# A planned attention and gated-FFN kernel: one constant per rule of the order replaced by tables indexed by score visit

## The chip, the cores and the metric

The kernel runs on one core of a Trainium2 chip. The metric is the time of one execution in device microseconds (us). Shorter is better. The kernel before has a median of 1091.6 us over three runs (1091.21 to 1092.62).

## The reference

One transformer block on 2048 tokens with 1024 features, all in bf16: multi-query attention (32 query heads of 32 features that share one key and one value head), then a feed-forward network (FFN) with a sigmoid gate.

```python
xn = layernorm(x)
q = (xn @ wq).reshape(B, S, 32, 32).transpose(0, 2, 1, 3)   # 32 heads of 32
k, v = xn @ wk, xn @ wv                                      # one head of 32
p = softmax(einsum("bhqd,bkd->bhqk", q, k) * 32 ** -0.5)
h = x + einsum("bhqk,bkd->bhqd", p, v).transpose(0, 2, 1, 3).reshape(B, S, 1024) @ wo
hn = layernorm(h)
out = h + (sigmoid(hn @ w_gate) * (hn @ w_up)) @ w_down      # 1024 -> 3584 -> 1024
```

## The kernel before, in words

**Tiles.** Tokens are cut into 16 tiles of 128 rows. Attention handles a token tile in two halves of 16 heads each, called `hf` in the code, so there are 32 halves. For each half the 2048 keys are cut into 16 key tiles `kt`. One pair (half, key tile) is a *score visit*; there are 512 of them (`NV`), counted by `v`.

**One visit** (`emit_S`). TensorE runs four matmuls of 32x128 by 32x512, each on its own quarter of the rows of the array. They put the scores of 16 heads into a pair of pairs of PSUM banks of the tile `S_ps`. ScalarE then runs two exponentials of 128x1024 from `S_ps` into a buffer `Pr` (L707). `S_ps` holds three such half-visits, so the scores of visit v cannot start before an exponential of the visit before has ended: the third matmul of a visit waits for the first exponential of the visit before, the first one for the second exponential of the visit before that. So TensorE can run ahead of ScalarE by one visit and no more.

**What follows a visit.** VectorE adds the exponentials of a half up in `acc` (L680). TensorE multiplies the exponentials with the values in two *P V bursts* per half of eight key tiles each (`mk_PV`), four matmuls at a time on the four quarters of the columns. At the end of a half it forms the sums of the exponentials in one burst of 32 short matmuls (`mk_SUM`), again on quarters of the columns. The sums are inverted, written to DRAM and read back spread out (`r_scratch`, `rb`), multiplied in (`OT`), and after two halves the token tile goes through the output projection `OP`, the second layernorm, a DMA transpose into `hnT`, the gate and up matmuls `GU` (14 groups of 8 matmuls, weights streamed from DRAM in slabs), a tanh on ScalarE per gate group (L989; the sigmoid is written with tanh), and the down projection `D` (56 matmuls, weights resident). All these use the whole array. At the start there are also the transposes `xT`, the key and value projection `KV`, and the query projection `Q0`, `Q1`, `Q`.

**Modes of the array.** The planner calls the scores "row" mode, P V and sums "col" mode, and everything else "dense" mode. A *switch* is a change of mode between two neighbouring matmuls.

**What sets the order.** No engine chooses anything at run time. Before the program is written, a planner in the file (class `Plan` and the loop at the end of the kernel) simulates all engines with a cost for each instruction (`t_act`, `t_dve`, `SWITCH`, DMA rates) and writes a fixed list of instructions for every engine, with semaphore waits between them. At each step of simulated time the loop decides what TensorE does next:

1. If the next visit can start (`s_known`) and ScalarE has less than `run` = 700 ns of work queued, the visit is issued. This interrupts whatever group of matmuls is under way.
2. Right after a col matmul, if the next visit can start within `swait` = 400 ns, TensorE is left idle until then.
3. A long dense group (`LONG`) may be put aside for a P V, SUM, OP or hT group, if at least `rmin` = 900 ns of it are left or another condition holds. P V and SUM may begin only in row mode, that is right after a visit, or where buffers are short (`in_row`, with `pv_few` = 4 and `sum_few` = 0).
4. Otherwise the next matmul of the current group is issued, or a new group is taken from the queues in a fixed order of classes (`PRIOS[qf]`, or `PRIO_D` when a down projection is due).

`early` = 240 ns in `s_known` says how far ahead of the end of an exponential the visit may be issued. The lists of VectorE, GpSimd and of the DMA queue on SyncE come out of the same simulation, so a different decision on TensorE moves the instructions of all engines.

Of the kernel before, what the change touches and what calls it, by code (L numbers as in the profile page):

```python
# [15 lines left out]
SEM = 75.0  # L16


TUNE = dict(early=240, look=500, ln_v=1, warm=70, late=300, ws0=1, ws1=1, parts0=3, parts1=4, lord=2, h_ord=2,
            ho=3, ho2=0, pvl1=0, pvl2=0, col_ok=0, pace0=310, swait=400, parts=2, raw=1, rl=0, nd=2, pc=16,  # L20
            rate=315, pace=265, xd=4, qf=1, dall=1, wo_late=1, nkn=3, few=0, rmin=900, hmin=1, h0=100, h1=250,
            hf=1.35, run=700, sum_few=0, pv_few=4, d_off=0, d_a=-1, d_b=1, eb=450, eq=1500)


class Op:
# [131 lines left out]


def t_act(n):
    return dict(occ=n / 1.2 + 58.0, lat=n / 1.2 + 186.0 + SEM)  # L160


def t_dve(n, rate=0.96, fix=158.0):
# [3 lines left out]
SWITCH = 108.0  # L167


def bass_sequential_preLN__grouped_kv_mqa__glu_gated_glu__prompt_kernel(  # L170
# [12 lines left out]
    Bsz, S, D = A_x.shape  # L183
# [3 lines left out]
    NT = S // P  # L187
# [14 lines left out]
    with ExitStack() as es:  # L202
# [66 lines left out]
        pl = Plan()  # L269
# [169 lines left out]
        queues = collections.defaultdict(collections.deque)  # L439
        PRIO_D = ["xT", "KV", "Q0", "PV", "SUM", "OP", "hT", "D", "GU", "Q1", "Q"]  # L440
        head = [["xT", "KV", "Q0"], ["KV", "Q0", "xT"], ["Q0", "KV", "xT"], ["KV", "xT", "Q0"]][TUNE["h_ord"]] + ["PV", "SUM", "OP", "hT"]
        PRIOS = [head + ["GU", "D", "Q1", "Q"], head + ["Q1", "Q", "GU", "D"], head + ["Q1", "GU", "Q", "D"]]

        def mm(o, l, r, start, stop, **kw):
            return lambda: PE.matmul(o, lhsT=l, rhs=r, start=start, stop=stop, **kw)  # L445

        def pe_op(fn, n, mode, deps, last_of_round=True):
            if mode != pl.pe_mode:
                pl.free["pe"] += SWITCH
                pl.pe_mode = mode  # L450
            if mode == "dense":
                occ = max(25.0, n / 2.4 + 2.4)
            else:
                occ = max(25.0, n / 2.4 + 2.4) - 10.5 if last_of_round else 3.5
            return pl.op("pe", fn, deps, occ=occ, lat=max(25.0, n / 2.4 + 2.0) + 170.0 + SEM)
# [49 lines left out]
        k_ev, v_ev = {}, {}  # L505
# [118 lines left out]
        NV = len(visits)  # L624
# [31 lines left out]
        def s_known(v, t):  # L656

            sd = s_ready(v)
            return sd is not None and known(sd, t) and (v < 1 or known([exps[2 * v - 2]], t + TUNE["early"]))

        late_adds = collections.defaultdict(list)
        RAW = tuple(range(TUNE["raw"])) + ((NH - 1,) if TUNE["rl"] else ())
# [60 lines left out]
        PARTS = [(), (), (0, 8, 16), (0, 5, 10, 16), (0, 6, 11, 16), (0, 4, 8, 12, 16), (0, 7, 16), (0, 6, 16), (0, 4, 10, 16), (0, 4, 8, 16)]  # L723

        def parts_of(hf):
            return PARTS[TUNE["parts" if hf > 1 else "parts0" if hf == 0 else "parts1"]]

        rb_ld = {}
        rs_ev = {}
# [2 lines left out]
        oun_ev = {}  # L732

        def in_row(few):
            return v_done[0] >= NV or pl.pe_mode == "row" or len(free_slots) <= few or TUNE["col_ok"] and pl.pe_mode == "col"

        def mk_SUM(hf):
            a = acc[:, hf % 2, :]

            def atoms(b):  # L740
                return [(mm(F_ps[DH * j:DH * (j + 1), b, 0:64], sel[:, bb, :], a[:, j * 512 + bb * 64:j * 512 + (bb + 1) * 64],
                            bb == 0, bb == 7, tile_position=(0, DH * j)), 64, "col" if j == 3 else "col-", [])
                        for bb in range(8) for j in range(4)]

            def after(b, last):
                sum_last[hf] = last
                flush_adds(hf + 2)
                rc = pl.op("dve", lambda: DVE.reciprocal(r_sb[:, :], F_ps[:, b, 0:64]),
                           [last, rd_ld.get(hf - 1)], prio=0, occ=480, lat=560 + SEM)
                rd_ld[hf] = dma(lambda: SP.dma_start(r_dram, r_sb[0:P:4, :]), "rd", 8192, [rc] + (rb_ld[hf - 1] if hf - 1 not in RAW else []), prio=0)  # L750
                rb_ld[hf] = [dma(lambda j=j: SP.dma_start(
                    rb[DH * j:DH * (j + 1), :], bass.AP(r_dram.tensor, r_dram.offset + 512 * j, [[0, DH], [1, 512]])),
                    "rb", 65536, [rd_ld[hf], ot_ev.get(hf - 1), ot_ev.get(0)], prio=0) for j in range(4)]
                finish(hf)
                return [rc]
            return Group("SUM", atoms, lambda: [add_op.get((hf, NT - 1)), c_sel], after, lambda: in_row(TUNE["sum_few"]))

        def finish(hf):

# [13 lines left out]
        def mk_PV(hf, part, sums=False):  # L773
# [36 lines left out]
                        finish(hf)  # L810
                return [oun_ev[(hf, part)]]

            lag = TUNE["pvl2"] if final else TUNE["pvl1"]

            def first():
                return [exp_of[(hf, kt, i)] for kt in kts[:len(kts) - lag] for i in range(2)] + [c_one if sums else v_ev.get(kt) for kt in kts]

            def gate():
                if part == 0 and hf >= 2 and not (hf - 2 in ot_ev and known([ot_ev[hf - 2]], pl.free["pe"])):
                    return False  # L820
                if sums and part == 0 and hf >= 2 and hf - 1 not in ot_ev:
# [25 lines left out]
        v_done = [0]  # L847
# [239 lines left out]
        def all_done(v):  # L1087

            v_done[0] = v
            if v == NV:  # L1090
                all_S[0] = True
                pl.t_last = pl.free["pe"]
                load_next([(s.rearrange("p (d f) -> p d f", d=4), rel) for s, rel in free_slots])

        def known(deps, t):
            return all(d is not None and d.end is not None and d.end <= t for d in deps)

        while True:
            t = pl.free["pe"]
# [203 lines left out]
```

## Time and profile before

| what | value |
|---|---|
| median of three runs | 1091.6 us |
| the profiled execution, span from first to last instruction | 1092.9 us, 1.3 us above the median |
| TensorE matmul busy | 1060.6 us, 97% |
| TensorE weight loads busy | 439.3 us, 40% |
| ScalarE busy | 1000.7 us, 92% |
| VectorE busy | 848.9 us, 78% |
| DMA queue busy share | 74.1% of 16 engines, 233.70 MB |
| first exponential starts, last one ends | 14.17 us, 1009.88 us |

No time of the profiled execution other than its span is given, so the span stands for it. The run has three stages. Up to about 140 us the projections run beside the first 64 visits. From about 200 us to the last exponential the trace repeats itself every 62.1 us, which is one token tile: 32 visits, one pass of the FFN, one output projection. After the last exponential comes a tail of 83.0 us without scores, with the rest of the FFN of two tiles and all of it for the last.

In the profile, PE is TensorE, PEld its weight loads, ACT ScalarE, DVE VectorE, POOL GpSimd, SP SyncE. A line such as `646.07 2.12 PE L445 MATMUL F_ps<-ring,hnT ... x9` of the timeline reads: from 646.07 us, 2.12 us long, nine matmuls with their source and target. The recorded length of one 512-column matmul (379 to 385 ns) includes the way through the array; the next one starts 216 ns after it, so costs are read from start to start.

### The profile page before, as it was taken

To read this page: it belongs to the slowest core of one execution; us is meant where nothing else is said; L and a number is where in the kernel's file an instruction comes from. 1 tells how busy PE (TensorE), PEld (TensorE's weight loads), DVE (VectorE), ACT (ScalarE), POOL (GpSimd) and SP (SyncE) were. 2 spreads that over 40 slices of the span, in tenths; PEclk is the share of its full clock that TensorE was granted. 3 is DMA by queue.
4 is the path that set the end of the run, shared out by engine and by line. 5 is a ranking of instruction groups with operands and counts; after the bars stand their busy time and mean duration, and the time that the engine had idled before them with its cause. 6 is when DMAs were issued, how large, how long until landed. Compare 5 with 4: busy or idle time off the path is not lost.

```text
span 1092.9 us, 23470 instructions
## 1 busy us (share of the span) xinstructions
PE 1060.6 (97%) x9314; PEld 439.3 (40%) x9454; DVE 848.9 (78%) x1054; ACT 1000.7 (92%) x1152; POOL 39.5 (4%) x61
## 2 busy tenths in 40 slices
PE   8999999999999999999999999999999999999998
PEld 6533465333333333333333333333333333333485
DVE  8989988787887878787887878787887878787311
ACT  4999999999999999999999999999999999999010
POOL 3300000000000000000000000000000000000000
PEclk9999999999999999999999999999999999999999
DMA  8893399868769595868858595877858586876992
GB/s 248 171 306 121 116 300 279 251 170 269 203 182 266 137 271 144 246 183 255 231 166 256 139 270 147 260 189 229 245 150 262 138 250 168 248 206 194 287 307 95
DMA packets 296509, 233.70 MB, mean 214 GB/s; under 512 B 99536, under 2 KB 282832, under 8 KB 296400
## 3 DMA queue, kind: packets, MB, share of 16 engines
q1 hardware_dynamic: 296400, 232.19, 74.1%
q8 instruction: 75, 1.23, 0.5%
q14 instruction: 34, 0.28, 0.1%
HBM read 203.82 MB, written 8.12 MB: 194 GB/s over the span
## 4 chain that ended last, share of the span: by engine, by line
ACT 67%; PE 22%; issue 5%; DVE 3%; DMA 2%; SPq 0%; DVEq 0%
ACT Pr L707 62%; PE F_ps L445 19%; ACT tnh L989 5%; PE S_ps L445 3%; DVE acc L680 1%; DMA hnT<-hn 1%; DMA r_scratch<-r_sb 1%; DMA zone<-ring 0%; DVE st L349 0%; DVE st L351 0%; DMA ring<-in_A_x_dram 0%; DMA rb<-r_scratch 0%; DVE hact L285 0%; DVE ring L393 0%; DVE OT L765 0%
## 5 line engine op out<-in xcount | busy, mean ns | idle before, releaser
L707 ACT ACTIVATE Pr<-S_ps 128x1024 bf16<-128x1024 f32 x1008 | 956.1, 1181 | 3.4 <-PE S_ps L445 3.4
L680 DVE TENSOR_TENSOR acc<-acc,Pr 128x2048 bf16<-128x2048 bf16 x431 | 524.7, 1217 | 45.4 <-ACT Pr L707 32.1
L445 PE MATMUL F_ps<-ring,hnT 128*128 128x512 bf16 x1506 | 366.8, 380 | 4.4 <-issue 4.1
L445 PE MATMUL F_ps<-zone,hact 128*128 128x512 bf16 x813 | 212.1, 381 | 6.5 <-issue 4.3
L445 PE MATMUL S_ps<-QTb,kT 32*128 32x512 bf16 x2048 | 206.8, 385 | 5.6 <-ACT Pr L707 4.7
L445 PEld LDWEIGHTS F_ps<-ring,hnT 128*128 128x128 bf16 x1536 | 134.6, 98 | 180.8 <-issue 43.0
L989 ACT ACTIVATE tnh<-F_ps 128x512 f32<-128x512 f32 x112 | 83.7, 747 | 60.3 <-PE F_ps L445 60.3
L445 PEld LDWEIGHTS S_ps<-QTb,kT 32*128 32x128 bf16 x2048 | 53.7, 91 | 205.0 <-ACT Pr L707 123.9
L445 PE MATMUL F_ps<-Pr,Vt 128*32 128x512 bf16 x2016 | 134.1, 382 | 0.0
L445 PEld LDWEIGHTS F_ps<-zone,hact 128*128 128x128 bf16 x896 | 75.5, 97 | 104.0 <-issue 34.6
L1010 DVE SCALAR_TENSOR_TENSOR act_s<-tnh,F_ps 128x512 bf16<-128x512 f32 x98 | 67.2, 686 | 58.4 <-PE F_ps L445 58.3
L445 PE MATMUL F_ps<-zone 128*128 128x512 bf16 (+3 forms) x573 | 72.9, 272 | 4.3 <-DVE ring L393 1.0
L445 PEld LDWEIGHTS F_ps<-Pr,Vt 128*32 128x32 bf16 x2016 | 43.0, 95 | 68.0 <-issue 28.6
L445 PE MATMUL F_ps<-wo_sb,OT 128*128 128x512 bf16 x241 | 62.3, 381 | 2.5 <-issue 1.7
L367 POOL TENSOR_TENSOR dsb<-zb,cst 128x1 bf16<-128x1 bf16 x18 | 23.0, 1280 | 964.6 <-DVE zb L364 964.6
L1057 DVE SCALAR_TENSOR_TENSOR h_sb<-F_ps,h_sb 128x512 bf16<-128x512 f32 x32 | 22.1, 692 | 40.4 <-PE F_ps L445 40.3
L445 PEld LDWEIGHTS F_ps<-zone 128*128 128x128 bf16 x584 | 39.0, 97 | 31.3 <-issue 9.2
L680 DVE TENSOR_TENSOR acc<-Pr 128x2048 bf16<-128x2048 bf16 x31 | 37.9, 1224 | 9.7 <-ACT Pr L707 9.7
L445 PE MATMUL F_ps<-hnT,ring 128*128 128x128 bf16 x576 | 37.7, 223 | 0.7 <-ACT tnh L989 0.7
L807 DVE TENSOR_TENSOR oun<-F_ps,oun 128x512 f32<-128x512 f32 x34 | 23.4, 688 | 18.9 <-PE F_ps L445 18.8
L445 PEld LDWEIGHTS F_ps<-hnT,ring 128*128 128x128 bf16 x576 | 33.6, 100 | 6.7 <-issue 5.9
L445 PEld LDWEIGHTS F_ps<-wo_sb,OT 128*128 128x128 bf16 x256 | 21.3, 97 | 34.0 <-issue 12.5
(81 smaller groups left out, 350.9 us busy)
## 6 DMA issues: line engine op xcount, KB each, us to landing
ring<-in_B_w_gate_dram SPq DMA_DIRECT2D x308, 256.0 KB, 3.9
ring<-in_B_w_up_dram SPq DMA_DIRECT2D x308, 256.0 KB, 4.0
rb<-r_scratch SPq DMA_DIRECT2D x124, 64.0 KB, 2.0
zone<-in_B_w_down_dram SPq DMA_DIRECT2D x14, 512.0 KB, 4.5
Pr<-in_B_w_gate_dram SPq DMA_DIRECT2D x20, 256.0 KB, 5.4
Pr<-in_B_w_up_dram SPq DMA_DIRECT2D x20, 256.0 KB, 5.0
ring<-in_A_x_dram SPq DMA_DIRECT2D x16, 256.0 KB, 6.4
h_sb<-in_A_x_dram SPq DMA_DIRECT2D x16, 256.0 KB, 2.9
```

Source lines behind the costliest of these rows:

```text
L367: g = pl.op("pool", lambda: POOL.tensor_tensor(out=dsb[:, ph, tk], in0=zb[:, ph, tk], in1=half[:, 0:k], op=ALU.pow), [f, c0], prio=0, **sl ...
L445: return lambda: PE.matmul(o, lhsT=l, rhs=r, start=start, stop=stop, **kw)
L680: add_op[(hf, kt)] = pl.op("dve", lambda: DVE.tensor_tensor(out=a, in0=in0, in1=slot, op=ALU.add), dp, prio=6, occ=1135, lat=1255)
L707: exps[u] = pl.op("act", lambda i=i, pb=pb: ACT.activation(out=slot[:, i * 1024:(i + 1) * 1024].rearrange("p (a b) -> p a b", a=2), in_=S_ ...
L807: oun_ev[(hf, part)] = pl.op("dve", lambda: DVE.tensor_tensor(out=o, in0=F_ps[:, b, :], in1=o, op=ALU.add), [last, oun_ev[(hf, part - 1)]] ...
L989: box["a"] = pl.op("act", lambda: ACT.activation(out=tnh[:, :], in_=F_ps[:, b, :], func=ACTF.Tanh, scale=0.5), [last, box.get("e")], prio= ...
L1010: e = pl.op("dve", lambda: DVE.scalar_tensor_tensor(out=so, in0=tnh[:, :], scalar=1.0, in1=F_ps[:, b, :], op0=ALU.add, op1=ALU.mult), [las ...
L1057: e = pl.op("dve", lambda: DVE.scalar_tensor_tensor(out=h_sb[:, t % NHB, sl], in0=F_ps[:, b, 0:DW], scalar=0.5, in1=h_sb[:, t % NHB, sl], ...
```

## The change

The scalar constants `early`, `few` (P V), `rmin`, `swait`, `run` are replaced by a lookup `kn(name)` in a table with one digit per visit, which selects from a short list of values (`VALUES`). The index is the number of visits issued so far; after the last visit it counts on by one for every 2 us of planned time. Four new choices are looked up the same way: `keep` (a visit may not interrupt a P V or SUM burst of which no more than this many ns are left), `lag` (a P V burst may begin before the exponentials of its last key tiles are known to have ended; TensorE then waits for them in the burst), `pri` (which order of classes is used), and `sm` (where the SUM burst may begin: 0 only after a visit, 1 only after a col burst, 2 anywhere). The default digit of each table is the old constant, or the old rule.

Some rules change for all visits. P V may now also begin right after a col burst (where `few` is above 0). SUM may no longer begin elsewhere only because buffers are short. The planner's cost of an activation falls from n/1.2 + 58 to n/1.2 + 50.7 ns, and a switch out of dense mode is costed 11.5 ns lower. `PARTS` gets further ways to cut a half into bursts, of which none is selected (`PARTS_OF` is empty).

No matmul, activation, vector operation or transfer is added or taken away. What changes is the order.

Visits of 512 whose digit differs from the default:

| table | early | keep | few | lag | rmin | pri | swait | sm | run |
|---|---|---|---|---|---|---|---|---|---|
| visits | 39 | 60 | 60 | 37 | 8 | 100 | 27 | 45 | 45 |

Together 260 visits have at least one such digit, 166 have one in `keep`, `few`, `lag` or `sm`. Of the first 64 visits 48 have one; in the blocks of 32 visits after that there are between 5 and 27. After the last visit all tables are at their default.

```diff
+VALUES = dict(early=(0, 80, 160, 240, 320, 450), keep=(0, 230, 450, 700), few=(0, 1, 2, 4, 16), lag=(0, 1, 2, 3),
+              rmin=(0, 500, 900, 1500), pri=(0, 1, 2, 3, 4, 5), swait=(0, 150, 400, 600, 900), sm=(0, 1, 2), run=(500, 700, 900))
+DEFAULT = dict(early=3, keep=0, few=3, lag=0, rmin=2, pri=0, swait=2, sm=0, run=1)
+CHOICES = {
+    'early': (
...
+    'sm': (
+        '0000000000000000000000000001000000000000222222220000000000000000222222220000000011111111000000000000'
...
+CHOICES = {n: [int(c) for c in d] + [DEFAULT[n]] * 100 for n, d in CHOICES.items()}
+PARTS_OF = {}
...
-    return dict(occ=n / 1.2 + 58.0, lat=n / 1.2 + 186.0 + SEM)
+    return dict(occ=n / 1.2 + 50.7, lat=n / 1.2 + 186.0 + SEM)
...
-        PRIOS = [head + ["GU", "D", "Q1", "Q"], head + ["Q1", "Q", "GU", "D"], head + ["Q1", "GU", "Q", "D"]]
+        PRIOS = [head + ["Q1", "Q", "GU", "D"], head + ["GU", "D", "Q1", "Q"], head + ["D", "GU", "Q1", "Q"],
+                 head[:-2] + ["GU", "D", "OP", "hT", "Q1", "Q"], head + ["Q1", "Q", "D", "GU"],
+                 head[:3] + ["SUM", "OP", "hT", "GU", "D", "Q1", "Q", "PV"]]
...
-                pl.free["pe"] += SWITCH
+                pl.free["pe"] += SWITCH if pl.pe_mode != "dense" else SWITCH - 11.5
...
-            return sd is not None and known(sd, t) and (v < 1 or known([exps[2 * v - 2]], t + TUNE["early"]))
+            return sd is not None and known(sd, t) and (v < 1 or known([exps[2 * v - 2]], t + kn("early")))
...
-            return v_done[0] >= NV or pl.pe_mode == "row" or len(free_slots) <= few or TUNE["col_ok"] and pl.pe_mode == "col"
+            return v_done[0] >= NV or pl.pe_mode == "row" or few > 0 and pl.pe_mode == "col" or len(free_slots) <= few
...
+            def sum_gate():
+                m = kn("sm")
+                return v_done[0] >= NV or m == 2 or m == 1 and pl.pe_mode == "col" or m == 0 and pl.pe_mode == "row"
...
-            return Group("SUM", atoms, lambda: [add_op.get((hf, NT - 1)), c_sel], after, lambda: in_row(TUNE["sum_few"]))
+            return Group("SUM", atoms, lambda: [add_op.get((hf, NT - 1)), c_sel], after, sum_gate)
...
-            lag = TUNE["pvl2"] if final else TUNE["pvl1"]
+            lag = 3
 
             def first():
-                return [exp_of[(hf, kt, i)] for kt in kts[:len(kts) - lag] for i in range(2)] + [c_one if sums else v_ev.get(kt) for kt in kts]
+                return [exp_of[(hf, kt, i)] for kt in kts[:len(kts) - kn("lag")] for i in range(2)] + [c_one if sums else v_ev.get(kt) for kt in kts]
...
-                return (hf in RAW or all((hf, max(kt, 1)) in add_op for kt in kts)) and in_row(TUNE["pv_few"])
+                return (hf in RAW or all((hf, max(kt, 1)) in add_op for kt in kts)) and in_row(kn("few"))
...
+        def index():
+            return v_done[0] if v_done[0] < NV else min(599, NV + int((pl.free["pe"] - pl.t_last) / 2000.0))
+
+        def kn(name):
+            return VALUES[name][CHOICES[name][index()]]
...
+        def keep_pv(t):
+            if cur is None or cur[0].cls not in ("PV", "SUM") or pl.pe_mode != "col":
+                return False
+            at = cur[1][cur_i:]
+            rem = sum(206.0 if a[2] == "col" else 3.5 for a in at)
+            return rem <= kn("keep") and all(known(a[3], t + 206.0 * (i // 4)) for i, a in enumerate(at))
...
-                if can_s and run - t < TUNE["run"]:
+                if can_s and run - t < kn("run") and not keep_pv(t):
                     emit_S(v)
...
-                        cur is not None and cur[1][cur_i][2] != "dense") and s_known(v, t + TUNE["swait"]) and run - t < TUNE["run"] + TUNE["swait"]:
+                        cur is not None and cur[1][cur_i][2] != "dense") and s_known(v, t + kn("swait")) and run - t < kn("run") + kn("swait"):
...
-                            len(cur[1]) - cur_i) * max(25.0, cur[1][cur_i][1] / 2.4 + 2.4) >= TUNE["rmin"]):
+                            len(cur[1]) - cur_i) * max(25.0, cur[1][cur_i][1] / 2.4 + 2.4) >= kn("rmin")):
...
-                    pr = PRIOS[TUNE["qf"]]
-                    if d_due and len(queues["GU"]) <= d_due[0] + TUNE["d_off"]:
+                    pr = PRIOS[kn("pri")]
+                    if kn("pri") == 0 and d_due and len(queues["GU"]) <= d_due[0] + TUNE["d_off"]:
                         pr = PRIO_D
```

More of the change, by code (lines that the diff above doesn't have):

```diff
@@ L16 @@
 SEM = 75.0
-TUNE = dict(early=240, look=500, ln_v=1, warm=70, late=300, ws0=1, ws1=1, parts0=3, parts1=4, lord=2, h_ord=2,
+TUNE = dict(keep=0, early=240, look=500, ln_v=1, warm=70, late=300, ws0=1, ws1=1, parts0=3, parts1=4, lord=2, h_ord=2,
             ho=3, ho2=0, pvl1=0, pvl2=0, col_ok=0, pace0=310, swait=400, parts=2, raw=1, rl=0, nd=2, pc=16,
@@ L22 @@
             hf=1.35, run=700, sum_few=0, pv_few=4, d_off=0, d_a=-1, d_b=1, eb=450, eq=1500)
+VALUES = dict(early=(0, 80, 160, 240, 320, 450), keep=(0, 230, 450, 700), few=(0, 1, 2, 4, 16), lag=(0, 1, 2, 3),
[3 more added lines that the diff above has]
+    'early': (
+        '3333333334333333333333333333333333333333222222223333333333333333333333333333333333333333333333333333'
+        '3333222222223333333333333333033333331111111133333333333333333333333333333333333333333333333333333333'
+        '3332333033303333333333333333333330333333353333333333333333333333333333333333333333333333333333533333'
+        '3333333333333333333333303333333333333333333333333333333333333333333333333333333333333333333333333333'
+        '1333333333333333353333333333333333333333234333333333333333333333333333333333333353333333333333333343'
+        '333333333333333333333333333333333333333333333333333333333333'),
+    'keep': (
+        '0000000000000203000000000000000000000000000000003333333333333333000000000000000011111111000000000000'
+        '0101000000000000000000000000000000000000000000000000000030000000000000000000222222220000000000002000'
+        '0000000000000000000000003001003000000030000000000000000000000000000000000000000000000000000010001000'
+        '2000000000000000000000000000000000000000000000000000000000000000000000000000000000000000000000000000'
+        '0000000000000000000000000000000001000000003030000000000000003000000102000000000000020000222222220000'
+        '000000000000000000000000000000000000000000000000000000000000'),
+    'few': (
+        '3333333333333433332303333333313333333333444444443333333333333333000000003333333333333333333333333333'
+        '3333333333333330333311111111333333334444444433333333333330033233333333333333333333333333333330333333'
+        '3333333333333333333333333333332333333333333333333333333333333333333333333333333333333333333333333333'
+        '3333333234133333333333333313000000003313333333333333333333333333333333433334333333333333333333333333'
+        '3313333333333333333333333333333333233333333333333033333333333333333333333333333333333333333333333333'
+        '333333333333333333333333333333333333333333333333333333333333'),
+    'lag': (
+        '0000000000000020000000000000000011111111000000000000000000000000000000000000000000000000000000003000'
+        '0000000000000000003011111111000000000000000000000000000000002000000300000000000000000000000000000000'
+        '0000000000000000000000000300000103000000000100030000000000203000000000000000000000000000020000000200'
+        '0000000000000000000000000000000000000000000000000000000000000000000000000000000000000000000000000000'
+        '0000000000000000000002000000000000000000000000000010000301000001000000000000000002000000000000002000'
+        '000000000000000000000000000000000000000000000000000000000000'),
+    'rmin': (
+        '2222222222222222222222222222222222222222222222222222222222222222222222222222222222222222222222222222'
+        '2222222222222022222222222222222222212222222222222222222222222222222222222222222222222222222222222222'
+        '2222222232222222222222222222222222022222222222222222222202222222222222222222222222222222222222222222'
+        '2222222222222222222222222222222222222222222222222222222222222222222222222222222222222222222222222222'
+        '2212222222222222222222222222222222222222222222222222222222022222222222222222222222220222222222222222'
+        '222222222222222222222222222222222222222222222222222222222222'),
+    'pri': (
+        '0000000000550000000000010000000011111111000000002222222211111111000000000000000000000000000000000000'
+        '0030333333330000020000000000001000003333333300000000002200000000000000000000000000000000000001000040'
+        '0002000000000440000000000000000040000005000000040000000000000000000000002222222200000000000000001000'
+        '0000000000040000000005000200000000000000202000000000000000000000000000050240000000005555555500000000'
+        '0000004000000000000000003333333300000000000000000000000000000000000052005555555500000000000000000000'
+        '000000000000000000000000000000000000000000000000000000000000'),
+    'swait': (
+        '2222222232222222222222222222222222222222222222222222222222222222222222222222222222222222222222222222'
+        '2222222222222222220222222222222212222222222222222222222222222223222222222222000000002222222222222222'
+        '2222222222222222222222222222222222212222222222222222222222232222222222222222222222222222022222222222'
+        '2222222222222222222222222222222222222222222222222222222222222222222222222222222222221111111122222222'
+        '3224222222222222222222222222222222222322222222222222222222222222222222222222222222222222222222220222'
+        '222222222222222222222222222222222222222222222222222222222222'),
+    'sm': (
+        '0000000000000000000000000001000000000000222222220000000000000000222222220000000011111111000000000000'
+        '0000000000000120000000000000000000000000000000000000000000000000000000000000000000000000000000000000'
+        '0020000000200000000000000000000000000000000000000000000000000000000000000000000000000000000010000002'
+        '0000000000000000000020100000000000000000100000000000000000000000000000000000000000002222222200000000'
+        '0000000000000000000000000000000010000000000020000000000000000000000000000000000000000000000000000002'
+        '000000000000000000000000000000000000000000000000000000000000'),
+    'run': (
+        '1111111111110112121221111111112122222222111111111111111111111111111111111111111111111111111111111101'
+        '1111222222221111011111111111111111011111111111111111111111111111111111111111111111111111111111111111'
+        '1121111111111112111111111111211111112111111111111111111111111121111111111111111111111111111111111111'
+        '1111111111111111111111121121111111111111111111111111111111111111111111111111111111111111111111111111'
+        '1111110111111111111111211111111111101111111111111111111111111111111111111111111121111111222222221110'
+        '111111111111111111111111111111111111111111111111111111111111'),
+}
@@ L721, in emit_S @@
                     queues["PV"].append(mk_PV(hf, parts_of(hf).index(kt + 1) - 1, True))
-        PARTS = [(), (), (0, 8, 16), (0, 5, 10, 16), (0, 6, 11, 16), (0, 4, 8, 12, 16), (0, 7, 16), (0, 6, 16), (0, 4, 10, 16), (0, 4, 8, 16)]
+        PARTS = [(), (), (0, 8, 16), (0, 5, 10, 16), (0, 6, 11, 16), (0, 4, 8, 12, 16), (0, 7, 16), (0, 6, 16), (0, 4, 10, 16), (0, 4, 8, 16), (0, 7, 14, 16), (0, 2, 9, 16), (0, 6, 13, 16), (0, 7, 12, 16), (0, 8, 14, 16)]
         def parts_of(hf):
-            return PARTS[TUNE["parts" if hf > 1 else "parts0" if hf == 0 else "parts1"]]
+            return PARTS[PARTS_OF.get(hf, TUNE["parts"]) if hf > 1 else TUNE["parts0" if hf == 0 else "parts1"]]
         rb_ld = {}
```

## The prediction

> **What bounds the kernel now.** First the busy times, then the waits of TensorE.
>
> ```profile
> PE 1060.6 (97%) x9314; PEld 439.3 (40%) x9454; DVE 848.9 (78%) x1054; ACT 1000.7 (92%) x1152; POOL 39.5 (4%) x61
> ```
>
> ```profile
> PE S_ps L445 <- ACT Pr L707: 4.7, 16, 0.5
> PE F_ps L445 <- DMA hnT<-hn: 1.5, 1, 1.5
> ```
>
> TensorE and ScalarE both look full. The two rows are the largest waits of TensorE's matmuls behind another engine's work after the start: 4.7 us and 1.5 us of 1092.9. Whether TensorE is truly full is read from the timeline of one period, from start to start, since its recorded ends are modelled.
>
> ```profile
> 646.07 2.12 PE L445 MATMUL F_ps<-ring,hnT 128*128 128x512 bf16 x9
> 648.11 0.40 PE L445 MATMUL S_ps<-QTb,kT 32*128 32x512 bf16 x4
> 648.44 1.47 PE L445 MATMUL F_ps<-ring,hnT 128*128 128x512 bf16 x6
> 649.84 0.39 PE L445 MATMUL S_ps<-QTb,kT 32*128 32x512 bf16 x4
> ...
> 667.78 0.40 PE L445 MATMUL S_ps<-QTb,kT 32*128 32x512 bf16 x4
> 668.11 0.60 PE L445 MATMUL F_ps<-zone,hact 128*128 128x512 bf16 x2
> 668.65 1.05 PE L445 MATMUL F_ps<-Pr,Vt 128*32 128x512 bf16 x16
> 669.63 0.40 PE L445 MATMUL S_ps<-QTb,kT 32*128 32x512 bf16 x4
> 669.95 1.05 PE L445 MATMUL F_ps<-Pr,Vt 128*32 128x512 bf16 x16
> 670.93 0.60 PE L445 MATMUL F_ps<-zone,hact 128*128 128x512 bf16 x2
> 671.47 0.39 PE L445 MATMUL S_ps<-QTb,kT 32*128 32x512 bf16 x4
> ```
>
> Nine dense matmuls take 9 x 0.216 = 1.94 us, yet the visit behind them starts 2.04 us after the first: the switch costs 0.10. The visit's four matmuls run at once, like one (0.216), and the dense work follows 0.33 later: switch 0.11. No other gap is left. So TensorE is the bound from the first visit on, and a mode switch costs it about 0.104 us.
>
> The second half shows what can be saved. The visit at 669.63 cuts a P V burst of eight key tiles in two, with dense work before and after: six switches (row-dense, dense-col, col-row, row-col, col-dense, dense-row) between the visits of 667.78 and 671.47. With the burst whole between two visits and the dense work in the other gap there are four.
>
> Counting changes of mode over the period from 638.46 to 700.56 gives 73: two for each of 32 visits, nine for gaps that hold both kinds. Counted over the whole timeline there are 1167. Two for each of 512 visits are 1024, so 143 are extra.
>
> ScalarE has little room beside it:
>
> ```profile
> 1004.58 0.71 ACT L989 ACTIVATE tnh<-F_ps 128x512 f32<-128x512 f32 x1
> 1005.06 4.82 ACT L707 ACTIVATE Pr<-S_ps 128x1024 bf16<-128x1024 f32 x5
> ```
>
> A tanh holds it 0.48 (start to start), an exponential (4.82 - 1.18) / 4 = 0.91, with the mean duration 1.18 from the group of L707; back to back, single starts lie 0.904 apart. A period needs 64 x 0.904 + 7 x 0.48 = 61.2 of its 62.1 us. From the first exponential (14.17) to the last one's end (1009.88) are 995.7 us. The exponentials need 1024 x 0.904 = 925.7, the 101 tanhs of this stage 48, the copies of L284 at the start 6 (groups of 3.4, 1.5, 0.5 and 0.6): 980. ScalarE caps a gain in this stage at 15.7 us.
>
> One place is different:
>
> ```profile
> 142.72 0.87 PE L445 MATMUL S_ps<-QTb,kT 32*128 32x512 bf16 x4
> 144.12 0.39 PE L445 MATMUL S_ps<-QTb,kT 32*128 32x512 bf16 x2 [0.53 <-ACT Pr L707]
> 145.04 0.39 PE L445 MATMUL S_ps<-QTb,kT 32*128 32x512 bf16 x2 [0.53 <-ACT Pr L707]
> 145.36 0.58 PE L445 MATMUL F_ps<-acc,sel 128*32 128x64 bf16 x32
> 145.88 2.53 PE L445 MATMUL F_ps<-hnT,ring 128*128 128x128 bf16 x22
> ```
>
> ```profile
> 144.00:146.00 2.00, 1.35 (x38) 0.74 (x39) 2.00 (x3) 2.00 (x4) 0.00 (x0) 0.86 1.08 344
> 146.00:148.00 2.00, 2.00 (x21) 2.00 (x20) 1.90 (x4) 1.74 (x2) 0.00 (x0) 0.50 1.09 351
> 148.00:150.00 2.00, 2.00 (x26) 1.23 (x24) 1.90 (x2) 1.02 (x2) 0.00 (x0) 0.79 1.03 335
> ```
>
> Around visit 67 TensorE has nothing but scores, waits 1.06 us for ScalarE, and then runs at a lowered granted clock (0.86, 0.50, 0.79 in the column after POOL): 0.28 + 1.00 + 0.42 = 1.7 us lost. The hole costs 2.8. The DMA share there is 1.03 to 1.09, the weights of the first FFN pass coming in.
>
> **The change, part by part.**
>
> *Fewer switches.* `keep` holds a visit back while a burst ends, `sm` lets the sums follow a P V burst, and the rule that P V may follow a col burst joins bursts; the other tables shift where visits fall among the groups. Ends: if only the 166 visits with a digit in the burst tables gain, 166/512 of 143 = 46 switches go, 4.8 us; if all extra ones go, 14.9. I take the 260 visits with any digit, 260/512 of 143 = 73 switches, 7.6 us, because a shifted visit moves a cut as well. No increase is taken in, since nothing in the default digits makes a cut likelier; the rivals price waits.
>
> *The hole at visit 67.* `sm` is 2 in visits 64 to 71 and `pri` puts GU before the remaining Q in 32 to 39 and 56 to 63, so sums or projections could fill it. Ends 0 and 2.8; neither row excludes either, I take half, 1.4.
>
> *The planner's costs.* Exponentials planned at 904 ns and not at 911 agree with the 0.904 above. It costs no instruction, but takes 7.3 x 64 = 0.47 us a period of slack out of the plan: a visit is now placed where ScalarE ends just in time. TensorE takes instructions in order, so behind a waiting visit stands all dense work, and behind that ScalarE's next exponentials. Ends: 0, as now, and the price in the third rival. I take 0, since the waits above are near nothing.
>
> *`lag`.* 37 visits allow a burst before its last exponentials have ended. This adds waits inside the burst, with the next visit queued behind. At the default digit the same exponentials are known before the burst begins, and the wait is over when it is reached. Price within the third rival.
>
> *SyncE and the other queues.* The same transfers, in another order. Where FFN work comes earlier, slabs are asked for earlier. In steady state the DMA share of a period is 0.74 and no matmul waits for a slab, so I put it at 0; that cover is missing near 145 us only (share 1.09), and its price is the end 0 in the hole's term. VectorE is busy 50.2 of 62.1 us in a period and GpSimd 1.5; moved additions have that room. If an addition is late, a `Pr` buffer is free later.
>
> *The tail.* After 1009.88 TensorE still works off part of FFN 13 and 14. Its waits there are 0.16, 0.52 and 1.50, and the chain of the last tile (sums to DRAM 5.5 us, back 2.8, transpose 6.6, together 15) lies beside about 36 us of that work (51 + 56 matmuls of D, 62 of GU, 0.216 each). With 9 us saved earlier 27 are left, still over 15, so the chain stays covered and the tail gives no term of its own.
>
> Sum: 7.6 + 1.4 = 9.0. Against the span, 1092.9 - 9.0 = 1083.9; less the 1.3 by which the span exceeds the median, 1082.6. The floor is 14.9 + 2.8 = 17.7, but ScalarE caps it at 15.7: 1091.6 - 15.7 = 1075.9; with the tail's 2.2 of waits gone too, 1073.7.
>
> **Two rules against it.** The Trainium skill, "ScalarE: Activation LUTs", section "What ACT_TABLE_LOAD costs", gives an activation 186 ns + 0.833 per element with about 93 of overlap: an estimate of 946 ns at 1024 elements. By that a period needs 64 x 0.946 + 7 x 0.52 = 64.2 us on ScalarE, more than the 62.1 it takes; ScalarE would be the bound already and the sum 0. The row of 0.91 decides. "Perfetto Trace Analysis", section "Identifying the Most-Contended Engine", calls matmul busy time a bad measure and wants weight loads looked at: by their 40% against ScalarE's 92% TensorE's switches would be free, again a sum of 0. The starts above, without a gap but the switches, speak otherwise.
>
> **The rivals.** *Hardly any change.* Default digits rule 252 visits, and a plan may fall back into the pattern of 73. Then only the start gains: 146 switches stand between 14 and 138 us, where 64 visits need 128, so 18 x 0.104 = 1.9 us: 1089.7. For it: 200 to 950 us repeats exactly. Against: digits stand in every block of 32 visits.
>
> *All of it.* Both floors are met: about 1075. For it: ScalarE's 61.2 us and TensorE's 62.1 - 0.94 (nine switches) meet. Against: few digits in several blocks.
>
> *Slower, by visits that wait.* The plan without slack lets TensorE arrive at visits before ScalarE is done. The 16 such waits now have a mean of 4.7/16 = 0.29 us. With 64 more, one visit in eight, 18.8 us come back: 1082.6 + 18.8 = 1101. It decides from 9.0/0.29 = 31 more waits on. Fewer do if one opens a hole like that at 145 us with its clock loss: 2.8 each. For it: a fixed list cannot react, and the slack was real. Against: only 16 such waits in 512 visits now, the longest 0.5 us.
>
> **How the numbers follow.** Fewer switches, near half of the extra: 0.60, 1077 to 1088, likeliest 1082.6. All: 0.10, 1073 to 1077. Hardly any: 0.11, 1088 to 1093, of which about half lies within 0.2% (2.2 us, about what a measurement here can tell from no change). Slower: 0.19, of which 0.01 falls within 0.2%. So faster 0.60 + 0.10 + 0.06 = 0.76, same 0.05 + 0.01 = 0.06, slower 0.18. The range 1074.5 to 1096 leaves out a few in a hundred below and the worse half of the slower case.
>
> **What would show it.** Right: about 1090 switches instead of 1167; periods of 61.2 to 61.8 us; more P V bursts of 32 matmuls in one piece; the last exponential ending near 1001; no clock under 0.9 at 145 us; a tail of about 83 us. Wrong: TensorE's waits behind L707 far above 4.7 us, a longer tail with waits on `hnT` or `rb`, or dips of the clock in several slices.

## The result, and the profile after

The changed kernel takes **1093.61 us** (median of 20 executions, 1091.89 to 1097.1). The kernel before, on the same chip, takes 1092.22 (1090.94 to 1093.88). The ratio is **1.0016, with a 95% interval of 1.0009 to 1.0023**: about as fast as before, rather a little slower, and 11.0 us above the forecast of 1082.6.

The profiled execution of the changed kernel has a span of 1091.3 us. The executions timed here list a span beside their time, and the time is 1.8 us the longer one in all of them. So the profiled execution of before, whose span of 1092.9 the prediction took as its time, really took about 1094.7: 2.5 us above the median of 1092.2. The two spans alone therefore point the wrong way (1.6 us faster), and part of this section is about why.

The busy times of the changed kernel, from its page:

```profile
PE 1059.5 (97%) x9325; PEld 441.5 (40%) x9454; DVE 848.3 (78%) x1053; ACT 1001.6 (92%) x1153; POOL 38.4 (4%) x61
```

Nothing moved by more than 2.2 us (the weight loads; the matmuls moved by 1.1, with 9314 and 9325 of 9454 recorded). The busy times cannot show what the order does. These rows of the waits of TensorE can (us in total, times, longest):

```profile
PE F_ps L519 <- DMA hnT<-hn: 1.7, 2, 1.0
PE F_ps L519 <- DMA zone<-in_A_wq_dram: 1.6, 2, 1.2
PE F_ps L519 <- DMA ring<-in_B_w_up_dram: 1.3, 3, 0.6
PE S_ps L519 <- ACT Pr L781: 1.2, 5, 0.3
```

The waits of scores for exponentials fell from 4.7 us in 16 to 1.2 in 5, and a row that was not among the large ones before stands in their place: matmuls that wait for a slab of `w_up`.

The stretch around 145 us, in the same three slices that the prediction shows of before (the two columns after POOL are the granted clock and the DMA share):

```profile
144.00:146.00 2.00, 2.00 (x12) 0.70 (x11) 2.00 (x3) 2.00 (x4) 0.00 (x0) 1.00 1.09 372
146.00:148.00 2.00, 2.00 (x21) 0.98 (x19) 1.79 (x3) 2.00 (x4) 0.00 (x0) 1.00 1.01 342
148.00:150.00 2.00, 2.00 (x61) 1.67 (x59) 2.00 (x3) 2.00 (x3) 0.00 (x0) 1.00 0.76 145
```

The clock is 1.00 throughout: the dip to 0.50 is gone.

The last exponentials, from the timeline of ScalarE:

```profile
999.14 3.93 ACT L781 ACTIVATE Pr<-S_ps 128x1024 bf16<-128x1024 f32 x4
1002.77 0.79 ACT L1067 ACTIVATE tnh<-F_ps 128x512 f32<-128x512 f32 x1
1003.25 7.64 ACT L781 ACTIVATE Pr<-S_ps 128x1024 bf16<-128x1024 f32 x8
```

The last one ends at 1010.89 (1003.25 + 7.64); before it was 1009.88. From 200 us on each 64 exponentials, counted in blocks from the first, take between 62.0 and 62.7 us, where before it was 62.0 to 62.1. The 61.2 to 61.8 us of the forecast are not there.

**An account of both traces.** Counted over the whole timeline, the mode switches went from 1167 to **1140**, 27 fewer and not 73. From visit to visit, a gap with six dense matmuls takes 1.728 us, which is seven steps of 0.2157 (the visit is one) and 0.2185 for two switches: 0.109 each. TensorE's waits I add up from the starts of its weight loads, which are all recorded: what a step takes beyond the usual one for its kind, where that is over 0.04 us, from 8 us on. This sees waits that the rows above give to "issue" or to the wrong engine.

| waits of TensorE, us | before | after |
|---|---|---|
| to 62 us | 5.6 | 6.5 |
| 62 to 124 us | 0.5 | 0.8 |
| 124 to 186 us | 5.0 | 2.6 |
| 186 to 248 us | 0 | 0.7 |
| 248 to 992 us | 1.2 | 5.5 |
| the rest | 2.8 | 1.9 |
| sum | 15.2 | 18.1 |

27 x 0.109 = 2.9 us of switches and 1.7 us of the dip are gained, and 18.1 - 15.2 = 2.9 us of waits are lost: a net gain of 1.7, against the 1.6 between the spans. So the account closes for the two profiled executions. As a formula, fitted to before alone, it reads: span = 948.8 + 0.109 x switches + waits + 1.7 where there is a dip. For the changed kernel it gives 1091.2 (measured 1091.3), and it is used on the experiments below.

The new waits of the steady stage are short and few. Here is the one at 735 us, in the timeline of TensorE:

```profile
734.38 0.40 PE L519 MATMUL S_ps<-QTb,kT 32*128 32x512 bf16 x4
734.71 1.04 PE L519 MATMUL F_ps<-ring,hnT 128*128 128x512 bf16 x4
736.30 1.24 PE L519 MATMUL F_ps<-ring,hnT 128*128 128x512 bf16 x5 [0.56 <-DMA ring<-in_B_w_up_dram]
737.47 0.39 PE L519 MATMUL S_ps<-QTb,kT 32*128 32x512 bf16 x4
```

Four matmuls from 734.71 should be followed by the next at 734.71 + 4 x 0.216 = 735.57. It starts at 736.30, 0.73 late (0.9 by the starts of the weight loads, which run ahead of the matmuls until the slab is missing, so that the account takes such a wait a little too long). What it waited for is in the SyncE queue, and in the chain of work that leads to that matmul:

```profile
728.41 0.37 SPq L1024 DMA_DIRECT2D ring<-in_B_w_up_dram  x1
728.82 1.26 SPq L970 DMA_TRANSPOSE hnT<-hn  x1
730.12 1.85 SPq L1024 DMA_DIRECT2D ring<-in_B_w_up_dram  x3
```

```profile
727.87 1.15 DVE acc L754
729.02 1.06 SPq L970
730.07 0.04 issue
730.12 0.67 SPq L1024
730.79 0.04 issue
730.83 5.33 DMA ring<-in_B_w_up_dram
736.17 0.14 issue
736.30 1.24 PE F_ps L519 x5
```

The issue of the slab stands in the queue behind the issue of a transpose, which lasts 1.26 us, and the slab then takes 5.33 us to land. Slabs are late three times in the stage: at 735, 798 and 922 us the matmul starts 0.7, 0.7 and 0.4 us late, 1.8 us in all. At 798 us the chain also runs through the issue of a transpose; at 922 us it does not. A wait of 0.4 us at 642 us is of another kind: the profile has it behind VectorE, which was reading a PSUM tile out (`oun`).

**The dip is not in every execution.** The mean clock that is listed with every timed execution of before is 0.998 in 26 of 59 and 1.000 in the rest; 3.41 us at half clock in 1092 are a mean of 0.998. Executions with 0.998 have medians 0.3 to 1.6 us higher. The changed kernel has 0.998 in 1 of 20. So a dip does cost before something, but in less than half of its executions, and its median cannot hold all of the 1.7 us that the profiled execution lost. That the dip of the others stands at the same hole is not shown: only the profiled execution has its place.

### The profile page after: what moved, and what is told of

Same layout as the page of the kernel before. It is cut to its first block, busy times and chain, and to the rows that moved or that the text cites. A ratio compares the mean times of both kernels' runs of the same rounds, so it can differ in the third digit from the quotient of the medians.

```text
span 1091.3 us, 23435 instructions
## 1 busy us (share of the span) xinstructions
PE 1059.5 (97%) x9325; PEld 441.5 (40%) x9454; DVE 848.3 (78%) x1053; ACT 1001.6 (92%) x1153; POOL 38.4 (4%) x61
## 4 chain that ended last, share of the span: by engine, by line
PE 47%; ACT 43%; issue 4%; DMA 3%; DVE 1%; SPq 1%; DVEq 0%
PE F_ps L519 40%; ACT Pr L781 39%; PE S_ps L519 7%; ACT tnh L1067 3%; DMA ring<-in_B_w_up_dram 1%; DMA zone<-in_A_wq_dram 1%; DVE acc L754 1%; DMA hnT<-hn 0%; DMA zone<-ring 0%; SPq L375 0%; SPq L970 0%; ACT h_sb L781 0%; ACT hact L781 0%; ACT QTb L781 0%; ACT hnT L781 0%
## 5 line engine op out<-in xcount | busy, mean ns | idle before, releaser
L781 ACT ACTIVATE Pr<-S_ps 128x1024 bf16<-128x1024 f32 x1008 | 956.4, 1179 | 3.7 <-PE S_ps L519 3.5
```

What stands on the lines that cost most here:

```text
L781: exps[u] = pl.op("act", lambda i=i, pb=pb: ACT.activation(out=slot[:, i * 1024:(i + 1) * 1024].rearrange("p (a b) -> p a b", a=2), in_=S_ ...
```

## The experiments

"Before" is the kernel before and "after" the changed one. Every ratio is to before on the same chip.

**1 and 2. Are late slabs the loss?** The same edit in both kernels: from the second FFN pass on, a slab brings half of its bytes. The order of all instructions stays.

```diff
-ops.append(dma(lambda q=q, view=view, gr=gr, W=W: SP.dma_start(
-    view[:, 2 * (q % 2):2 * (q % 2) + 2, :],
-    W[256 * q:256 * q + 256, gr * SW:(gr + 1) * SW].rearrange("(a p) f -> p a f", p=P)),
+ops.append(dma(lambda q=q, view=view, gr=gr, W=W, h=2 if p == 0 else 1: SP.dma_start(
+    view[:, 2 * (q % 2):2 * (q % 2) + h, :],
+    W[256 * q:256 * q + 128 * h, gr * SW:(gr + 1) * SW].rearrange("(a p) f -> p a f", p=P)),
```

> The changed kernel with every order as it is; from the second FFN pass on a slab transfer brings only half of its bytes (one of two row blocks; the other half of the slab stays as it was, so the FFN is computed from stale weights there). Theory A (in the changed order TensorE waits for late weight slabs, some 3 to 5 us in all, and these waits also make the spread of its runs): the waits for slabs vanish, the time falls by 3 to 5 us against the changed kernel to 1088 to 1090, and the runs lie as close as those of the kernel before. Theory B (the visits wait for ScalarE because the plan has no slack): waits for slabs are not what is lost, the time stays within 1 us of 1093.

> The control: the kernel before with the same half slabs from the second FFN pass on. In its trace no matmul of the repeating stage waits for a slab, so theory A expects no change, within 1 us of 1092. If this one falls by 3 us or more as well, less DMA traffic helps in some other way, and the first run proves nothing about slabs.

After with half slabs: 1091.41 us (1090.59 to 1092.15), ratio 0.9992 [0.9983, 1.0001]. Before with half slabs: 1092.13 (1091.02 to 1092.69), ratio 0.9994 [0.9986, 1.0003]. So the changed kernel gains 0.24% (2.6 us) by the edit and the kernel before 0.06%. No row of a wait for `ring` is left in the changed kernel's list; its waits sum to 15.8 us and its executions lie within 1.6 us instead of 5.2. Late slabs cost the changed kernel about 2 us, less than the 3 to 5 expected. They probably make most of its spread; the control narrows too, but less, from 3.1 us (21 executions) to 1.7 (11). And without late slabs the changed kernel is only 0.7 us faster than before, not 9. Most of what was forecast is missing elsewhere.

**3 and 4. The two halves of the change alone.** The change has two parts: the digits, and the planner's costs (an activation 7.3 ns cheaper, a switch out of dense mode 11.5 ns cheaper). Run 3 is after with all digits at their default, run 4 is before with the new costs.

```diff
-CHOICES = {n: [int(c) for c in d] + [DEFAULT[n]] * 100 for n, d in CHOICES.items()}
+CHOICES = {n: [DEFAULT[n]] * 660 for n, d in CHOICES.items()}
```

```diff
-    return dict(occ=n / 1.2 + 58.0, lat=n / 1.2 + 186.0 + SEM)
+    return dict(occ=n / 1.2 + 50.7, lat=n / 1.2 + 186.0 + SEM)
...
-                pl.free["pe"] += SWITCH
+                pl.free["pe"] += SWITCH if pl.pe_mode != "dense" else SWITCH - 11.5
```

> The changed kernel with every digit at its default: the new rules and the new planner costs alone. Theory C (what the digits buy is 27 mode switches of 0.109 us, 3 us, and the lower price of a switch in the plan buys nothing on the chip): the program has 1174 switches, 7 more than before, so about 0.8 us slower than before if nothing waits, 1093; the digits then are worth the difference to the changed kernel. Rival D (the new costs alone let ScalarE's stage end earlier, as the plan says, by 7 us): 1085.

> The kernel before with the two new planner costs (activation + 50.7, switch out of dense 11.5 ns cheaper) and nothing else. 1179 switches instead of 1167. Theory C: 12 x 0.109 = 1.3 us slower, 1093 to 1094, more if slabs come late. Rival D: the last exponential ends 7 us earlier and the time falls to 1085.

Default digits: **1102.97 us** (1101.03 to 1104.27), ratio 1.0095 [1.008, 1.011]. Before with the new costs: **1103.23** (1102.89 to 1104.4), ratio 1.0101 [1.0087, 1.0115]. Every expectation missed: I had no theory in which the costs alone lose 10 us. The two agree, so no loss is seen from the rules that the change alters for all visits. Run 4 has 1179 switches and 24.0 us of waits in its trace, run 3 1174 and 26.1 (against 1167 and 15.2 before). The waits are spread over all kinds. These are the lines of run 4 that weigh most, first from the list of waits, then from the timelines at 166 us and in the tail:

```profile
PE S_ps L445 <- ACT Pr L707: 5.8, 18, 0.5
PE F_ps L445 <- DMA ring<-in_B_w_up_dram: 2.6, 3, 1.3
```

```profile
166.49 0.50 PE L445 MATMUL S_ps<-QTb,kT 32*128 32x512 bf16 x4
167.52 0.39 PE L445 MATMUL S_ps<-QTb,kT 32*128 32x512 bf16 x2 [0.53 <-ACT Pr L707]
168.44 0.39 PE L445 MATMUL S_ps<-QTb,kT 32*128 32x512 bf16 x2 [0.53 <-ACT Pr L707]
168.75 0.23 PE L445 MATMUL F_ps<-hnT,ring 128*128 128x128 bf16 x1
169.44 1.05 PE L445 MATMUL F_ps<-Pr,Vt 128*32 128x512 bf16 x16 [0.46 <-ACT Pr L707]
...
1043.92 1.89 PE L445 MATMUL F_ps<-Pr,hnT 128*128 128x512 bf16 x8 [0.76 <-DMA Pr<-in_B_w_gate_dram]
1047.08 1.89 PE L445 MATMUL F_ps<-ring,hnT 128*128 128x512 bf16 x8 [1.28 <-DMA ring<-in_B_w_up_dram]
```

A hole like that of visit 67 stands at another place, with a dip of the clock behind it, and the tail waits for slabs. The account gives 948.8 + 128.5 + 24.0 + 1.7 = 1103.0 for run 4 (span 1101.1) and 1104.6 for run 3 (1102.5). It is 2 us high because the dip is in it twice: the steps that it slows here are long, and 1.3 and 1.5 us of them are among the waits already. Without the 1.7 it gives 1101.3 and 1102.9. So the loss is in switches and waits of TensorE.

So under the new costs the digits bring 1102.97 to 1093.61, **9.4 us** (8.6 by the two ratios to before, 1.0095 and 1.0016). That the forecast for the digits and the hole was 9.0 is luck: they remove 34 switches, 3.7 us, and not 73; most of the rest is waits, which fall from 26.1 to 18.1 us between the two traces. And this is one way to split the change. The other, the changed kernel's tables under the old costs, was not run, so how much of the gain belongs to the digits alone stays open.

**5 and 6. Is it these costs, or any other costs?** Theory F: the constants of before, and the digits of after, fit one plan each, and any other price leads to another plan that they do not fit. Rival G: it is these new prices, the lower price of a switch above all, and the digits keep their worth under any other. Both kernels get an activation that is 0.5 ns dearer, which is 1/14 of the change.

```diff
-    return dict(occ=n / 1.2 + 58.0, lat=n / 1.2 + 186.0 + SEM)
+    return dict(occ=n / 1.2 + 58.5, lat=n / 1.2 + 186.0 + SEM)
```

```diff
-    return dict(occ=n / 1.2 + 50.7, lat=n / 1.2 + 186.0 + SEM)
+    return dict(occ=n / 1.2 + 51.2, lat=n / 1.2 + 186.0 + SEM)
```

> The kernel before; only the planner's price of an activation is 58.5 instead of 58.0 ns above n/1.2. On the chip an activation costs what it did, so only the order changes. Theory F (the old constants are fitted to one plan, and any change of a price throws the order off it): 1181 switches instead of 1167 are 1.5 us, and with waits of 5 to 10 us more the time is 1098 to 1104, like the kernel before with the two new prices (1103.2). Rival G (the two new prices cost 10 us because the lower price of a switch is wrong): half a nanosecond in the other price changes nothing, 1091 to 1094.

> The changed kernel with its tables; only the planner's price of an activation is 51.2 instead of 50.7 ns above n/1.2. Theory F: the tables are fitted to one plan as well; off it, TensorE gets 1148 switches instead of 1140 (0.9 us) and more waits than with default digits, 1103 to 1112. Rival G: the digits are rules that hold for a visit whatever the plan, so they keep their worth: 1092 to 1096.

Before with 58.5: **1102.49 us** (1100.74 to 1104.85), ratio 1.0100 [1.0082, 1.0118]. After with 51.2: **1108.63** (1107.96 to 1112.78), ratio 1.0162 [1.0139, 1.0185]. Half a nanosecond in the planner costs 10 us in the one and 15 us in the other: G falls, and F has both numbers right. The switches rise to 1181 and 1148, the waits to 20.1 and 32.7 us. The rows have no single culprit; first the largest two of before with 58.5 that stand behind another engine's work, then those of after with 51.2:

```profile
PE S_ps L445 <- ACT Pr L707: 4.4, 10, 1.0
PE F_ps L445 <- DVE act_s L1010: 4.0, 12, 0.3
```

```profile
PE S_ps L519 <- ACT Pr L781: 5.3, 17, 0.5
PE F_ps L519 <- DMA hnT<-hn: 1.7, 1, 1.7
PE F_ps L519 <- ACT tnh L1067: 1.6, 2, 0.9
PE F_ps L519 <- DVE oun L885: 1.5, 3, 0.8
```

The plan shows this loss without the chip. The planner of each kernel file gives a simulated end of its list: 1088.0 us before, and 1097.2 with 58.5; 1078.3 after, and 1097.6 with 51.2. So the planned ends are 9.3 and 19.2 us later, though 1024 exponentials that are 0.5 ns dearer add only 0.5 us of work. But F's "any" goes too far. With prices half a nanosecond *lower*, 57.5 and 50.2, the planned ends stay within 0.03 us; these two were not run on the chip. The changed kernel's tables under the old costs, not run either, would end at 1092.3, 4.4 us behind before. A small change of a price can throw the order off, and need not. That the constants of before were chosen for their plan is likely, but not on record.

**7. Digits without new costs.** If F holds, digits fitted under the costs of before should keep their gain. This kernel has the rules of the change, the old costs, and tables of its own, chosen so that the planner's own end of the list is early (the tables are left out here).

```diff
-    return dict(occ=n / 1.2 + 50.7, lat=n / 1.2 + 186.0 + SEM)
+    return dict(occ=n / 1.2 + 58.0, lat=n / 1.2 + 186.0 + SEM)
...
-                pl.free["pe"] += SWITCH if pl.pe_mode != "dense" else SWITCH - 11.5
+                pl.free["pe"] += SWITCH
```

> The changed kernel's rules with the old planner costs (58.0; 108 for every switch) and other digits, fitted to these costs. 1144 switches instead of 1167 (2.5 us less), and the plan itself idles TensorE 3.1 us less than the plan of the kernel before (9.7 for 12.8). Theory F (digits buy what the plan says, as long as the plan's costs are those under which orders ran without unplanned waits): 5 to 6 us faster than before, 1086 to 1087. Rival H (digits drive the plan so close that late slabs and visits eat it): within 1.5 us of before, with 3 us or more of added waits in the trace.

**1090.68 us** (1087.4 to 1093.24), ratio 0.9985 [0.9976, 0.9994]: faster than both kernels, by 1.5 us against before, but the 5 to 6 that theory F expected are not in its median; only its best execution is near (1087.4). That one was profiled: span 1085.6, 1144 switches, 11.95 us of waits, account 1085.4.

**8 and 9. Costs nearer to the measured ones.** An activation at 50.7, every switch at 110 ns (measured 109), and two sets of tables fitted to that (left out here).

```diff
-SWITCH = 108.0
+SWITCH = 110.0
...
-                pl.free["pe"] += SWITCH if pl.pe_mode != "dense" else SWITCH - 11.5
+                pl.free["pe"] += SWITCH
```

> The changed kernel's rules, digits fitted to costs that agree with the trace: an activation at the new 50.7, every switch at 110 (the trace has 218 ns for a pair, the changed kernel's plan 204.5). 1141 switches (2.8 us less). Theory F: repriced at 110 the plan of the kernel before would be 2.3 us longer; this one is 6.1 us below that, so about 1086. Rival H: activations planned without slack make visits wait, 1089 to 1094.

> As the run before, other digits fitted to the same costs; 1128 switches, 39 fewer than before (4.3 us), with the same planned end within 0.1 us. Theory F: 1086, like it, because only the planned end counts. A theory that counts switches alone would have it 1.4 us faster than that run.

1093.53 us (1092.52 to 1094.31), ratio 1.0011 [1.0002, 1.002], and 1095.87 (1094.38 to 1096.53), ratio 1.0032 [1.002, 1.0044]. The second has the fewest switches of all, 1128, and is the slowest of the fitted ones: its waits sum to 22.0 us, those of run 8 to 19.4. Theory F had 1086 for both, so its further claim, that fitted digits buy what the plan says, fails here: the planned ends of the two agree within 0.1 us and the times differ by 2.3. A fitted plan can promise fewer switches and give them back as waits that the plan does not hold. Rival H has the number of run 8 (1089 to 1094), but not its mechanism: visits wait for exponentials 0.9 us in run 8 and 0.5 in run 9, against 4.7 before. Of run 9 these are the large rows:

```profile
PE F_ps L519 <- DMA zone<-ring: 1.8, 2, 1.6
PE F_ps L519 <- DMA zone<-in_A_wq_dram: 1.7, 2, 1.2
PE F_ps L519 <- DVE oun L885: 1.5, 2, 1.2
```

**10. What run 7 loses between its best execution and its median.** Run 7 with the half slabs of runs 1 and 2, on another chip, with before beside it there.

> The kernel of the old costs with digits of its own (same order of all instructions), in which from the second FFN pass on every weight slab of gate and up brings half of its bytes, so half of the weights of those passes are left out of the computation. It asks what lifts the median of that kernel (1090.7) above the 1087.4 of its best execution, and what spreads it over 5.8 us. If it is slabs that come late in some executions (theory S, as with the changed kernel, where the same edit took 2.2 us off the median and two thirds of the spread): median 1087 to 1088.5, spread under 2.5 us. If it is something else, such as the start, exponentials or the clock (rival H): median 1090 to 1091.5, spread still 4 us or more.

**1088.28 us** (1087.22 to 1089.41), ratio 0.9959 [0.9946, 0.9973]: 0.26% less than run 7, and 2.2 us of spread (5 executions) for 5.8 (12). That is theory S: slabs that land late in some executions. Where the half slab leaves work out, the kernel is no better version; it shows what the order of run 7 would give if its slabs came in time. What makes a slab late in one execution and not in the next stays open.

## Why the prediction was wrong

**The step that failed** is the term *The planner's costs*: "I take 0, since the waits above are near nothing." Its ends were "0, as now, and the price in the third rival", as if the costs only moved slack within the same order. They do not: the loop decides by comparing simulated times, and a price changed by 0.5 ns can already lead to another order (runs 5 and 6). The order of before is one at which its constants do well, and both other prices that were run on it put it 10 us behind. The costs alone measured **+10.5 us** (run 4, 1103.23 against 1092.70 beside it), the digits under them -9.4 by the medians; together +1.1, for the measured +1.4. With the first set to 0 and the second near the forecast sum of -9.0, this term is nearly the whole miss. The third rival did price the lost slack, as visits that wait for ScalarE, which is not what came. That 50.7 (904 ns) agrees better with the trace than 58 (911 ns) says nothing of what another plan costs; runs 8 and 9, with costs nearer to the measured ones, were no faster than before.

**Fewer switches**, 73 x 0.104 = 7.6 us, was the second step that failed. The price was right (0.109 by a cleaner gap). The number was not: 27, worth 2.9. The sentence "nothing in the default digits makes a cut likelier" is where it broke: under the new costs the default digits have 1174 switches and not 1167, so the digits remove 34. The share 260/512 was no measure of what a digit does; a visit with a digit need not remove a cut, and in run 9 39 switches less came with 6.8 us more waits than before.

**The hole at visit 67**, 1.4 taken of 2.8. The mechanism was right: the hole is filled, the waits from 124 to 186 us fell by 2.4 us and the dip's 1.7 are gone. That is more than the term, in this pair of executions. The hole was read too small: by the starts of the weight loads its three waits are 0.5, 0.9 and 0.9 us, 2.3 and not 1.06, as the recorded ends of the matmuls hide a part; with the dip it cost 4.0 and not 2.8. But the dip is in under half of the executions of before, so the median had less to give, and "less the 1.3 by which the span exceeds the median" also hid that the profiled execution took 2.5 us more than the median. The difference of 9.0 did not depend on that.

***SyncE and the other queues*, put at 0.** The clause "no matmul waits for a slab" was true of before only. The DMA share of the stage hardly changed (0.74 to 0.77 from 200 to 1005 us); what changed is when a slab is asked for, in two of the three late cases behind a transpose. It cost about 2 us and much of the spread (runs 1 and 2). A mean share is no cover for a transfer that is issued late.

***`lag`* and the third rival.** Its waits behind exponentials did not come: 5 of them, 1.2 us, against 16 and 4.7. Slower by visits that wait was the wrong mechanism for the right sign. In runs 3, 4 and 6, where the plan fits badly, such waits are 17 to 20, 5.3 to 6.3 us, a smaller part than the sum of the others.

**The tail** was right at about 0: 80.4 us of span after the last exponential (1091.3 - 1010.89) for 83.0, with waits of 1.9 for 2.8. That TensorE is the bound was right as well: the account with switches and waits of TensorE alone gives the spans of the profiled executions to within 1.4 us, once the dip of runs 3 and 4 is counted once.

**The two rules** that were weighed would each have said 0, which is near the result, but by luck: the runs do not bear out their reasons. Exponentials still start 0.904 us apart, and run 7's span shrank to 1085.6 with the same number of exponentials, so ScalarE was not the bound at 946 ns each. And switches are not free beside 40% of weight loads: in the account they have their 0.109 each.

## What to carry to other kernels

Where a planner writes the order, a change of its costs is a change of the whole order: test the costs alone and a change too small to matter, before anything is put down to the rules that came with them, and expect that constants which do well on one plan may lose on the next: here they did at each other price that was run. A plan's own gain (here 9.6 us earlier by the planner's end, of which 466 exits from dense mode at 11.5 ns are 5.4 us of mere repricing) is no measured gain; count switches and waits in the trace instead. A planned loss at unchanged work is a warning, though: 9.3 and 19.2 us in the plans of runs 5 and 6 came as 10 and 15 on the chip. Ask of each profiled execution where it stands among the timed ones before two of them are subtracted.

## What the runs showed of the hardware

- A dip of the granted clock in the middle of a busy kernel, 3.41 us at half speed in the profiled execution of before, followed a stretch in which TensorE had nothing but scores and waited 2.3 us in three waits, the longest 0.9 us. The Trainium skill, "TensorE: Matmul & The Clock Gate", section "HAM oscillation — how this bites in real kernels", puts it as a rule that there be no idle gaps of TensorE above about 3.4 us. Here shorter waits came before a dip. The waits alone do not decide it: in the profile of run 2 the same three waits stand near the same place (143.8 to 146.2 us), and the clock is 1.00 from 144 to 150 us. A mean clock of 0.998, as one such dip gives, stands in 26 of 59 executions of before.
- A pair of mode switches costs 0.2185 us with dense work between visits, and 0.226 with a P V burst.
- The same order of instructions spreads over 5.2 us with whole slabs (20 executions) and over 1.6 us with half ones (11), in the changed kernel. The kernel before, which has no wait for a slab in its profiled repeating stage, goes from 3.1 to 1.7 us by the same edit. So late slabs can be a part of what spreads the times, and not all of the narrowing can be put down to them.
